# Three real products for each complex one in a gated mix of a state-space scan and a long convolution: products, one spectrum and the work between them moved

## The chip, the cores and the metric

The kernel runs on one core of one Trainium2 chip. The time of a run is the device time of one execution in microseconds (us). Three runs of the kernel before took 379.05, 379.08 and 380.93 us, so its median is 379.08 us.

## The reference, cut to what matters

Two sequence models read the same input x (2048 steps of 1024 channels, bf16). Model A is a diagonal complex state-space scan; model B is a causal convolution of each channel with a kernel as long as the sequence. A gate mixes them.

```python
def _A_ref(x, Lambda_re, Lambda_im, B_re, B_im, C_re, C_im, log_dt, Dskip):
    ...
    Bu = jnp.einsum("bld,pd->blp", x + 0j, B_bar)
    for t in range(L):
        h = Lam_bar[None, :] * h + Bu[:, t, :]
    ...
    y = 2.0 * jnp.einsum("blp,dp->bld", hseq, Cmat).real + x * Dskip[None, None, :]

def _B_ref(q, k, v, shift_k, ssm_k, ssm_D):
    for t in range(ks):
        k_shift = k_shift + k_pad[:, t:t + S, :] * shift_k[:, ks - 1 - t][None, None, :]
    kv = k_shift * v
    ...
    y_f = kv_f * kf_f[None, :, :, :]
    y = irfft2(y_f)[:, 0, :S, :].astype(bfloat16)
    y = y + kv * ssm_D[None, None, :]
    return q * y

g = _sigmoid((x * gate_w).sum(-1, keepdims=True))
return g * _A_ref(x, ...) + (1 - g) * _B_ref(x, k, v, ...)
```

The change concerns `kv_f * kf_f`, the product of two complex spectra in model B.

## The kernel before

**Model B by chunks.** The 1024 channels are cut into 8 chunks of 128 (`NC` = 8). For each chunk the convolution kernel (K) and the sequence kv (V) are cut into four blocks of 512 steps, and each block is taken to a spectrum of 512 frequencies by TensorE, as matmuls with tables of cosines (`CF`) and sines (`SF`, `NCF`). A spectrum tile has 128 partitions and, on each, [part c: cosine or sine][block b: 4][frequency and channel: 512], 4096 bf16 values. `fwd_K` (line 636) makes K's spectrum (PSUM tile `psk`, copied by ScalarE into a tile called BT) and `fwd_V` (line 674) makes V's (`psv`, copied into `Vh`); each does so in four pieces (`fi`), each with its own PSUM tile and one copy by ScalarE. K's spectrum needs each block to be overlapped with the block before it. For chunks 0 to 6 that is done by TensorE: 16 more matmuls with 384 columns. For chunk 7 (`c == NC - 1`) these are left out and VectorE does it in `overlap_K` (line 667) with six additions of 512 elements.

**The products.** Block b of the result is the sum over a of K(a) times V(b - a), complex, so there are 4 + 3 + 2 + 1 complex products for each frequency. `products` (line 687) is a generator, and each `yield` ends a step that the main loop places. It makes four real products for each complex one: both parts of K times both parts of V, in `acc`, `wkh` (`WK`) and a scratch tile `t`, then adds them up. A part of the sums (128x3072 elements, 768 KB) is added by a DMA with an accumulating write, issued from GpSimd's queue (`gather`, line 127: `acc<-wkh`), except in chunk 7. At its end it writes the result as sum and difference of two halves back into the place of V's spectrum (`Vh<-acc`, two instructions). `inverse` (line 769) is TensorE's inverse transform of it (`psz`): the first eight matmuls wait for the first of the two `Vh` instructions, the next eight for the second. ScalarE copies `psz` to `cv`, which goes to DRAM.

**The rest of a chunk.** `taps` (four-tap filter on TensorE), `times_v` (line 603; three steps: VectorE multiplies `ks` by v; TensorE mirrors it and ScalarE copies the mirror to `lo`; VectorE makes `ev<-ks,lo` and GpSimd's queue issues an accumulating DMA `ks<-lo`), and folds of K (`foldk`, or `mirror_K` for chunks 2 and 7). `fwd_V` needs `ev` in its first two matmuls of a piece and the landed `ks<-lo` in the next two.

**Model A between them.** `Bu` makes tiles of B times x. For the first four calls they are spread over the chunks as filler for TensorE by `parts` (line 1187): `Bu_tile` (calls 0 and 1; steps `odd`, `even`, then a step `lamd` that writes once more into the PSUM tile of `even`) and `Bu_halves` (calls 2 and 3; `odd`, `even`, and a step that does nothing). An `odd` or `even` step is 16 matmuls of 256 columns. After the chunks come the other calls, the scans on VectorE and the products with C (`psy`) on TensorE.

**What sets the order.** The helpers `mm`, `tt`, `act`, `move`, `gather` chain each instruction behind the one before it on its engine, so every engine runs in the order of the program's text, and the main loop (line 1190, `for c in range(NC - 1)`) is that order written out. In iteration c the order is, roughly: the inverse of chunk c - 1, the first steps of `products(c)`, K's spectrum of chunk c + 1, the fold and taps of chunk c + 2, the rest of `products(c)`, V's spectrum of chunk c + 1. PSUM is one pool of four tiles (line 82): a matmul group waits until ScalarE has copied out the tile that had its place.

All engine instructions issued through the helpers bear line 95 in the profile, so tiles are told apart by name.

Of the kernel before, what the change touches and what calls it, by code (L numbers as in the profile page):

```python
# [9 lines left out]
ALU = mybir.AluOpType  # L10
# [10 lines left out]
def kernel(  # L21
# [42 lines left out]
    NC = D // 128  # L64
# [33 lines left out]
    def mm(o, l, r, first, last):  # L98
        put("pe", nc.tensor.matmul, o, lhsT=l, rhs=r, start=first, stop=last)
# [587 lines left out]
    def products(c, h=0, home=u4, by_dma=True):  # L687

        K, Vt = (x[c][h].rearrange("p c b f d -> p c b (f d)") for x in (KH, VH))
        w = K.shape[3]  # L690
        A = sums[:, :, h * 2048:h * 2048 + 8 * w].rearrange("p k (c b x) -> p k c b x", c=2, x=w)

        def mult(a, t):

            if len(t.shape) == 2:
                t = t.rearrange("p (k y) -> p k y", k=2)
            t = t.rearrange("p k (c b x) -> p k c b x", c=2, x=w)
            k_ = bc(K[:, :, a:a + 1], [128, 2, 8 - 2 * a, w])
            v_ = bc(Vt[:, :, 0:4 - a].rearrange("p c b x -> p c (b x)")[:, None], [128, 2, 2, (4 - a) * w])
            tt(t, k_, v_, ALU.mult)  # L700
            return t

        n1 = WK[:, h * 3072:h * 3072 + 12 * w].rearrange("p (k c b x) -> p k c b x", k=2, c=2, b=3)

        def first(k):

            for f in range(2 if c == 0 and h == 0 else 1):
                x = slice(f * 128, f * 128 + 128) if c == 0 and h == 0 else slice(0, w)
# [5 lines left out]
        if by_dma:  # L714
            first(0)
            yield
            second(0)
            gather(A[:, 0, :, 1:], n1[:, 0])
            yield
            first(1)  # L720
            yield
            second(1)
            if c > 0:
                yield
            tt(A[:, 1, :, 1:], A[:, 1, :, 1:], n1[:, 1], ALU.add)
        else:
            mult(0, sums)
            yield
            mult(1, WK[:, 0:6144])
            yield  # L730
            tt(A[:, :, :, 1:], A[:, :, :, 1:], n1, ALU.add)
        if c > 0:
            yield
        if c > 0:
            n3 = mult(3, home([128, 4 * w], BF16, "t"))
            n2 = WK[:, 3072:7168].rearrange("p (k c b x) -> p k c b x", k=2, c=2, b=2)
            for k in (1, 0):
                tt(n2[:, k], bc(K[:, k:k + 1, 2:3], [128, 2, 2, w]), Vt[:, :, 0:2], ALU.mult)
            yield
            for k in (1, 0):  # L740
                tt(n2[:, k, :, 1:], n2[:, k, :, 1:], n3[:, k], ALU.add)
            tt(A[:, 1, :, 2:], A[:, 1, :, 2:], n2[:, 1], ALU.add)
            yield
            for i in (0, 1):
                tt(A[:, 0, i, 2:], A[:, 0, i, 2:], n2[:, 0, i], ALU.add)
            yield
        else:
            n2 = mult(2, home([128, 8 * w], BF16, "t"))
            n3 = mult(3, home([128, 4 * w], BF16, "t"))
            yield  # L750
            tt(n2[:, :, :, 1:], n2[:, :, :, 1:], n3, ALU.add)
            tt(A[:, 1, :, 2:], A[:, 1, :, 2:], n2[:, 1], ALU.add)
            yield
            tt(A[:, 0, :, 2:], A[:, 0, :, 2:], n2[:, 0], ALU.add)
            yield
        tt(A[:, 1, 1], A[:, 0, 0], A[:, 1, 1], ALU.subtract)
        tt(A[:, 1, 0], A[:, 0, 1], A[:, 1, 0], ALU.add)
        if c == 0 and h == 0:
            return
        t2 = sums[:, 1]  # L760
        if c > 0:
            lo, hi = (A[:, 1, :, :, i * 256:(i + 1) * 256] for i in range(2))
        else:
            lo, hi = (t2[:, i * 2048:(i + 1) * 2048].rearrange("p (c b x) -> p c b x", c=2, x=256) for i in range(2))
# [400 lines left out]
    step(turns)  # L1165
    taps(1, dg1)
    step(columns)
    p0 = products(0, 0)
    steps(p0, 3)
    run(columns)  # L1170
    step(sp)
# [12 lines left out]
            load_t(CT[pi][:, c], src[:, pi * 128:(pi + 1) * 128])  # L1184

    old = none
    parts = (None for i in range(4) for b in Bu(i) for _ in b)
    tiles = (b for i in (4, 5) for b in Bu(i))

    for c in range(NC - 1):  # L1190
        n, nn = c + 1, c + 2
        if c == 0:
            load("kn", 2)
            load("kT", 2)
            load("v", 2)
            load_BT(0, 0)
            load_xT(0, (0,))
            p1 = products(0, 1)
# [24 lines left out]
            run(apart)  # L1223
            continue
# [9 lines left out]
        if c == 6:  # L1234
            step(parts)
        run(back)
        step(tv)
        steps(prod, 4)
# [10 lines left out]
        if c == 2:  # L1249
            step(parts)  # L1250
        fwd_K(n, (0, 1))
        if c in (2, 6):
            step(parts)
        fwd_K(n, (2, 3))
        if c == 1:
            lam_diag(0, lam_pool, True)
        if c == 4:
            step(parts)
        if c == 6:
            run(sp)  # L1260
            s5p["Q"] = s5p["wu"]
# [3 lines left out]
        if nn < NC:  # L1265
            if not by_channel(nn):
                fk = mirror_K(nn)
            step(fk)
            if c < 5:
                step(fk)  # L1270
            if c == 4:
                step(parts)
            if c == 1:
                load_BT(1, 0, True)
            elif c < 5:
                load("v", nn, True)
            step(parts)
            taps(nn, dg)
            if c == 5:
                load("v", nn)  # L1280
                load_xT(2, held=True)
            if nn + 1 < NC:
                load("kT", nn + 1, True)
                load("kn", nn + 1)
                apart = spread(nn + 1)
                step(apart)
                if c == 1:
                    load_BT(1, 1)
                elif c in (2, 3):
                    load_xT(1, (3 - c,))  # L1290
                run(apart)
        step(prod)
        run(fk)
        run(prod)
        if n == NC - 1:
            overlap_K(n)
        if nn < NC:
            tv = times_v(nn)
            step(tv)
            step(parts)  # L1300
        else:
            run(next(tiles))
            CT[0] = ld.tile([128, 2, D], BF16, name="CTa", tag="ld")
# [4 lines left out]
            run(next(tiles))  # L1308
            run(next(tiles))
        fwd_V(n, (0, 1))  # L1310
        if c < 6 and c != 4:
            step(parts)
            if c in (1, 3):
                step(parts)
        fwd_V(n, (2, 3))
        if c in (4, 5):
            step(parts)
        if c == 1:
            lam_diag(1, lam_pool)
        old = tabs  # L1320
# [291 lines left out]
```

## Time and profile before

| | |
|---|---|
| three runs | 379.08 us median (379.05 to 380.93) |
| the profiled execution's own time | 381.19 us |
| its span, first to last instruction | 379.4 us |
| mean granted TensorE clock | 0.998 |
| TensorE (PE) busy | 373.6 us, 2469 matmuls |
| VectorE (DVE) busy | 368.0 us, 596 instructions |
| ScalarE (ACT) busy | 303.6 us, 465 instructions |
| GpSimd (POOL) busy | 78.0 us, 106 instructions |

A row of a timeline gives start, duration, engine, line, operation, output and inputs, shape and count, and in brackets the idle time before it with what ended it. A row of the chain of waits gives start, duration and what. A row of the groups gives the group with its count, then its busy time in us and the mean duration of one in ns. Matmuls overlap in a pipeline, so the distance between starts tells their rate, and not their durations. A row of DMA issues gives the transfer, the queue, the count, the size and the time from the issue to landing. The profiled execution took 1.8 us more than its span.

### The profile page before, as it was taken

What the parts mean: (1) busy time and instruction counts of PE and PEld (TensorE: products, weight loads), DVE (VectorE), ACT (ScalarE), POOL (GpSimd) and SP (SyncE); (2) the same over time, 40 slices, a digit from 0 to 9 for tenths busy, and PEclk for the clock granted to TensorE, in tenths of its full rate; (3) what the DMA queues carried; (4) which work ended last, traced back from release to release, by engine and by line L of the source; (5) the groups of instructions that cost most, each with busy time, mean ns of one, the idle gap of its engine ahead of it and who ended that gap; (6) DMA issues with size and microseconds to landing.
All of it is one profiled execution on the core that took longest, in us unless ns stands there. A gap on an engine that the chain in (4) does not pass through costs nothing.

```text
span 379.4 us, 6680 instructions
## 1 busy us (share of the span) xinstructions
PE 373.6 (98%) x2469; PEld 202.4 (53%) x2469; DVE 368.0 (97%) x596; ACT 303.6 (80%) x465; POOL 78.0 (21%) x106
## 2 busy tenths in 40 slices
PE   8999999999999999999999999999999999999996
PEld 5666457566584756754454444444445444444444
DVE  8899999999999999999999999999999999999984
ACT  5779998998989999777999699977979968936301
POOL 4011020020301102022012014122426322532000
PEclk9999999999999999999999999999999999999999
DMA  7879999999999998999999999946999998997223
GB/s 168 162 117 232 209 210 209 226 214 212 223 191 193 214 192 177 187 208 151 188 209 226 228 199 246 211 70 119 185 248 157 268 248 178 189 244 125 57 83 111
DMA packets 125827, 70.99 MB, mean 187 GB/s; under 512 B 104601, under 2 KB 107553, under 8 KB 125794
## 3 DMA queue, kind: packets, MB, share of 16 engines
q1 hardware_dynamic: 112416, 45.90, 55.4%
q0 software_dynamic: 12256, 24.38, 37.8%
q10 hardware_dynamic: 1122, 0.28, 0.4%
q8 instruction: 19, 0.31, 0.3%
q14 instruction: 14, 0.11, 0.1%
HBM read 15.48 MB, written 8.39 MB: 63 GB/s over the span
## 4 chain that ended last, share of the span: by engine, by line
PE 91%; DMA 6%; ACT 2%; SPq 0%; issue 0%; DVE 0%; ACTq 0%
PE psy L95 29%; PE both L95 22%; PE psk L95 10%; PE taps L95 6%; PE psv L95 6%; PE psz L95 5%; PE even L95 4%; PE odd L95 3%; DMA kT<-in_B_k_dram 3%; PE foldk L95 3%; DMA kT<-kT 2%; DMA kB<-kT 1%; ACT Vh L95 1%; PE p L95 1%; PE mirror L95 1%; ACT hr L95 1%
## 5 line engine op out<-in xcount | busy, mean ns | idle before, releaser
L95 PE MATMUL psy<-CT,U 128*128 128x512 bf16 (+1 forms) x426 | 93.2, 374 | 0.0
L95 PEld LDWEIGHTS <-U 128*128 128x128 bf16 x492 | 48.1, 98 | 55.6 <-issue 0.3
L95 PEld LDWEIGHTS <-BT 128*128 128x128 bf16 x544 | 50.5, 98 | 33.5 <-issue 0.2
L95 DVE TENSOR_TENSOR wkh<-BT,Vh 128x2048 bf16<-128x2048 bf16 (+3 forms) x31 | 44.7, 1460 | 0.0
L95 POOL DMA_DIRECT2D U<-Q x26 | 27.1, 1053 | 82.8 <-ACT Q L95 24.8
L95 DVE TENSOR_TENSOR acc<-BT,Vh 128x4096 bf16<-128x4096 bf16 (+3 forms) x19 | 37.0, 1950 | 0.6 <-ACT Vh L95 0.6
L95 ACT ACTIVATE Q<-U,lam 128x512 bf16<-128x512 bf16 (+1 forms) x60 | 35.0, 626 | 2.6 <-issue 1.9
L95 PE MATMUL both<-xT,BT 128*128 128x512 bf16 x160 | 35.3, 379 | 0.0
L95 ACT ACTIVATE Vh<-psv 128x1024 bf16<-128x1024 f32 x32 | 30.7, 1032 | 5.6 <-PE psv L95 5.6
L95 DVE TENSOR_TENSOR_SCAN A<-rv,init,A 128x256 bf16<-128x256 f32 x48 | 34.4, 736 | 0.0
L95 DVE TENSOR_TENSOR acc<-acc,wkh 128x1024 bf16<-128x1024 bf16 (+4 forms) x30 | 32.7, 1130 | 0.1
L95 ACT ACTIVATE BT<-psk 128x1024 bf16<-128x1024 f32 x31 | 30.1, 1037 | 2.3 <-PE psk L95 2.2
L95 ACT ACTIVATE U<-both 128x512 bf16<-128x512 f32 x44 | 24.3, 594 | 8.1 <-PE both L95 7.8
L95 POOL DMA_DIRECT2D acc<-wkh x8 | 9.8, 1219 | 100.2 <-DVE wkh L95 100.2
L95 PE MATMUL psk<-eok,SF 128*128 128x384 bf16 (+1 forms) x120 | 28.5, 354 | 0.0
L95 PEld LDWEIGHTS <-SF 128*128 128x128 bf16 x184 | 18.0, 98 | 18.8
L95 ACT ACTIVATE BT<-psy,gcols 128x1024 bf16<-128x1024 f32 (+1 forms) x6 | 6.3, 1043 | 24.7 <-issue 14.0
L95 PE MATMUL taps<-dg,kT 128*128 128x128 bf16 (+1 forms) x352 | 23.3, 219 | 1.0 <-DMA kT<-kT 0.5
L95 PE MATMUL psz<-Vh,CI 128*128 128x512 bf16 x64 | 24.3, 379 | 0.0
L95 PE MATMUL psz<-Vh,SI 128*128 128x512 bf16 x64 | 24.3, 379 | 0.0
L95 PEld LDWEIGHTS <-kT 128*128 128x128 bf16 x352 | 22.8, 104 | 2.7 <-DMA kT<-in_B_k_dram 1.4
L95 DVE TENSOR_TENSOR U<-U,trn 128x512 bf16<-128x512 bf16 (+1 forms) x60 | 22.0, 391 | 0.1
(225 smaller groups left out, 784.0 us busy)
## 6 DMA issues: line engine op xcount, KB each, us to landing
U<-Q POOLq DMA_DIRECT2D x26, 256.0 KB, 5.2
acc<-wkh POOLq DMA_DIRECT2D x6, 768.0 KB, 8.3
cv_scr<-cv SPq DMA_DIRECT2D x16, 256.0 KB, 3.7
kn<-in_B_ssm_k_dram SPq DMA_DIRECT2D x5, 512.0 KB, 4.4
v<-in_B_v_dram SPq DMA_DIRECT2D x5, 512.0 KB, 5.0
out_dram<-m SPq DMA_DIRECT2D x8, 256.0 KB, 4.6
BT<-cv_scr SPq DMA_DIRECT2D x7, 256.0 KB, 7.2
out_dram<-BT SPq DMA_DIRECT2D x7, 256.0 KB, 2.0
```

Of the source, the lines that this page charges most:

```text
L95: i = f(*a, **kw)
```

## The change

For chunks 1 to 7, `products` makes three real products for each complex one. With V's parts V0 and V1 and K's parts K0 and K1: `both[0]` is K0 (V1 - V0), `both[1]` is K1 (V1 + V0) and `third` is (K0 + K1) V0. The parts of the result are `third - both[1]` and `third + both[0]`. It first makes `Vp` (V1 - V0 and V1 + V0) in `WK`, and uses V1's place in `Vh` as scratch once V1 has been used. `products_0` keeps the old code for chunk 0.

K's spectrum of chunk 3 is made without the 16 overlapping matmuls too (`apart_K`), and `overlap_K` is two additions of 1536 elements that write into `WK` (`K_later`) instead of six of 512 in place. It runs before the last step but one of `products(c)`, not behind it, and for these two chunks the second product goes to the place of K's spectrum, which for chunk 3 is then the DMA's source (chunk 7 has no such DMA).

`times_v(nn)`'s first step (`ks<-ks,v`) comes before the last two steps of `products(c)`, not behind them. `in_parts` drops the steps that do nothing and takes the third call's tiles in the order odd, odd, even, even. The table `count` places the steps: chunk 1 as before, chunk 2 seven steps (before: five), chunks 3, 4 and 5 three each (before: four, five, four), chunk 6 none (before: two).

```diff
+    apart_K = (3, NC - 1)
+    K_later = {}
...
-                    mm(ps[:, cc], tab[:, mt, fsl], eo[:, cc, mt], mt == 0, c == NC - 1 and mt == 1)
-                for mt in range(0 if c == NC - 1 else 2):
+                    mm(ps[:, cc], tab[:, mt, fsl], eo[:, cc, mt], mt == 0, c in apart_K and mt == 1)
+                for mt in range(0 if c in apart_K else 2):
...
-        K = KH[c][0]
-        for b in (3, 2, 1):
-            tt(K[:, 0, b], K[:, 0, b], K[:, 1, b - 1], ALU.add)
-            tt(K[:, 1, b], K[:, 1, b], K[:, 0, b - 1], ALU.subtract)
+        K = KH[c][0].rearrange("p c b f d -> p c b (f d)")
+        t = K_later[c] = WK[:, 4096:7168].rearrange("p (c b x) -> p c b x", c=2, b=3)
+        tt(t[:, 0], K[:, 0, 1:], K[:, 1, 0:3], ALU.add)
+        tt(t[:, 1], K[:, 1, 1:], K[:, 0, 0:3], ALU.subtract)
...
+    def products(c, home=u4, by_dma=True):
...
+        both, third, S = blocks(area[:, 0:4096], 4, 2), blocks(area[:, 4096:6144], 4), blocks(area[:, 6144:], 4)
+        Vp = blocks(WK[:, 0:4096], 4, 2)
+        n1 = blocks(WK[:, 4096:], 3, 2)
+        free = Vt[:, 1].rearrange("p b x -> p (b x)")
+        m1, n2 = blocks(free[:, 0:1536], 3), blocks(free, 2, 2)
+        V0 = Vt[:, 0]
...
+        if c in K_later:
+            n1, later = K[:, :, 1:], K_later[c]
+            def Kb(b):
+                return later[:, :, b - 1:b] if b else K[:, :, 0:1]
+        def pair(o, b, n):
+            tt(o, bc(Kb(b), [128, 2, n, w]), Vp[:, :, 0:n], ALU.mult)
+        def one(o, b, n):
+            tt(o, bc(S[:, b:b + 1], [128, n, w]), V0[:, 0:n], ALU.mult)
+        tt(Vp[:, 1], Vt[:, 1], Vt[:, 0], ALU.add)
+        tt(Vp[:, 0], Vt[:, 1], Vt[:, 0], ALU.subtract)
+        yield
+        pair(both, 0, 4)
+        yield
+        pair(n1, 1, 3)
+        if by_dma:
+            gather(both[:, :, 1:], n1)
+        if c in K_later:
+            tt(S[:, 0], K[:, 0, 0], K[:, 1, 0], ALU.add)
+            tt(S[:, 1:], later[:, 0], later[:, 1], ALU.add)
+        else:
+            tt(S, K[:, 0], K[:, 1], ALU.add)
+        yield
+        t = home([128, 4 * w], BF16, "t")
+        n3, m2, m3 = blocks(t[:, 0:1024], 1, 2), blocks(t[:, 1024:], 2), S[:, 0:1]
+        pair(n3, 3, 1)
+        one(third, 0, 4)
+        yield
+        one(m1, 1, 3)
+        one(m2, 2, 2)
+        if not by_dma:
+            tt(both[:, :, 1:], both[:, :, 1:], n1, ALU.add)
+        one(m3, 3, 1)
+        tt(third[:, 1:], third[:, 1:], m1, ALU.add)
+        yield
+        pair(n2, 2, 2)
+        tt(m2[:, 1:], m2[:, 1:], m3, ALU.add)
+        tt(n2[:, :, 1:], n2[:, :, 1:], n3, ALU.add)
+        tt(third[:, 2:], third[:, 2:], m2, ALU.add)
+        yield
+        tt(both[:, :, 2:], both[:, :, 2:], n2, ALU.add)
+        yield
+        tt(both[:, 1], third, both[:, 1], ALU.subtract)
+        tt(both[:, 0], third, both[:, 0], ALU.add)
...
-    parts = (None for i in range(4) for b in Bu(i) for _ in b)
+    def in_parts():
+        for i in range(4):
+            for b in ([tile_ for pair_ in [Bu(2)] for _ in range(2) for tile_ in pair_] if i == 2 else Bu(i)):
+                for _ in range(1 if i == 2 else 3 if i < 2 else 2):
+                    step(b)
+                    yield
+    parts = in_parts()
+    count = {1: "D1 F1 G2", 2: "A1 B1 C1 D1 E2 F1", 3: "A1 D1 F1", 4: "C1 D1 F1", 5: "D1 F1 H1"}
+    def at(place):
+        for x in count.get(c, "").split():
+            if x[0] == place:
+                steps(parts, int(x[1:]))
...
+        at("A")
         fwd_K(n, (0, 1))
+        at("B")
         fwd_K(n, (2, 3))
...
+        at("C")
...
+            at("D")
             taps(nn, dg)
+            at("E")
...
         run(fk)
-        run(prod)
-        if n == NC - 1:
-            overlap_K(n)
         if nn < NC:
             tv = times_v(nn)
             step(tv)
-            step(parts)
+        step(prod)
+        if n in apart_K:
+            overlap_K(n)
+        run(prod)
+        if nn < NC:
+            at("F")
...
         fwd_V(n, (0, 1))
+        at("G")
         fwd_V(n, (2, 3))
+        at("H")
...
-    prod, back = products(c, 0, room, False), inverse(c - 1)
+    prod, back = products(c, room, False), inverse(c - 1)
     run(old)
-    steps(prod, 3)
+    steps(prod, 4)
```

More of the change, by code (lines that the diff above doesn't have):

```diff
@@ L685, in fwd_V, with products_0 @@
             act(of_tile(VH[c], fi), ps, func=ACT.Copy, scale=2.0 / 1024.0)
-    def products(c, h=0, home=u4, by_dma=True):
+    def products_0(h):
+        c = 0
         K, Vt = (x[c][h].rearrange("p c b f d -> p c b (f d)") for x in (KH, VH))
@@ L705, in first @@
         def first(k):
-            for f in range(2 if c == 0 and h == 0 else 1):
-                x = slice(f * 128, f * 128 + 128) if c == 0 and h == 0 else slice(0, w)
+            for f in range(2 if h == 0 else 1):
+                x = slice(f * 128, f * 128 + 128) if h == 0 else slice(0, w)
                 tt(A[:, k, :, :, x], bc(K[:, k:k + 1, 0:1, x], [128, 2, 4, x.stop - x.start]), Vt[:, :, :, x], ALU.mult)
@@ L712, in second @@
             tt(n1[:, k], bc(K[:, k:k + 1, 1:2], [128, 2, 3, w]), Vt[:, :, 0:3], ALU.mult)
[L714 to L755, printed above, removed]
+        first(0)
@@ new lines, in products_0 @@
+        yield
+        second(0)
+        gather(A[:, 0, :, 1:], n1[:, 0])
+        yield
+        first(1)
+        yield
+        second(1)
+        tt(A[:, 1, :, 1:], A[:, 1, :, 1:], n1[:, 1], ALU.add)
+        n2 = mult(2, u4([128, 8 * w], BF16, "t"))
+        n3 = mult(3, u4([128, 4 * w], BF16, "t"))
+        yield
+        tt(n2[:, :, :, 1:], n2[:, :, :, 1:], n3, ALU.add)
+        tt(A[:, 1, :, 2:], A[:, 1, :, 2:], n2[:, 1], ALU.add)
+        yield
+        tt(A[:, 0, :, 2:], A[:, 0, :, 2:], n2[:, 0], ALU.add)
@@ L756, in products @@
+        yield
         tt(A[:, 1, 1], A[:, 0, 0], A[:, 1, 1], ALU.subtract)
         tt(A[:, 1, 0], A[:, 0, 1], A[:, 1, 0], ALU.add)
-        if c == 0 and h == 0:
+        if h == 0:
             return
         t2 = sums[:, 1]
-        if c > 0:
-            lo, hi = (A[:, 1, :, :, i * 256:(i + 1) * 256] for i in range(2))
-        else:
-            lo, hi = (t2[:, i * 2048:(i + 1) * 2048].rearrange("p (c b x) -> p c b x", c=2, x=256) for i in range(2))
+        lo, hi = (t2[:, i * 2048:(i + 1) * 2048].rearrange("p (c b x) -> p c b x", c=2, x=256) for i in range(2))
@@ L1167 @@
     step(columns)
-    p0 = products(0, 0)
+    p0 = products_0(0)
     steps(p0, 3)
@@ L1197 @@
             load_xT(0, (0,))
-            p1 = products(0, 1)
+            p1 = products_0(1)
             fwd_K(n, (0, 1))
@@ L1256 @@
             lam_diag(0, lam_pool, True)
-        if c == 4:
-            step(parts)
+        at("C")
         if c == 6:
@@ L1270 @@
                 step(fk)
-            if c == 4:
-                step(parts)
             if c == 1:
@@ L1299 @@
             step(tv)
-            step(parts)
+        step(prod)
[4 more added lines that the diff above has]
+            at("F")
         else:
@@ L1310 @@
         fwd_V(n, (0, 1))
[L1311 to L1314, printed above, removed]
+        at("G")
         fwd_V(n, (2, 3))
-        if c in (4, 5):
-            step(parts)
+        at("H")
         if c == 1:
```

23 lines of the change are left out of this document (17 added, 6 removed).

## The prediction, made before the changed kernel was run

> **What bounds the kernel now.** I read the page's busy shares first, then the chain of waits, then timelines by engine where the two busiest engines meet.
>
> ```profile
> PE 373.6 (98%) x2469; PEld 202.4 (53%) x2469; DVE 368.0 (97%) x596; ACT 303.6 (80%) x465; POOL 78.0 (21%) x106
> PE 91%; DMA 6%; ACT 2%; SPq 0%; issue 0%; DVE 0%; ACTq 0%
> ```
>
> The chain that ended last is 91% TensorE, and VectorE is 97% busy: two engines are full, so a gain needs both. TensorE's order behind chunk 5 is untouched, so the question is when it gets there. The places where it meets VectorE are the inverse transforms: their first matmul (call its start P of chunk c) waits for the first of the two `Vh<-acc` instructions.
>
> ```profile
> 47.11 2.29 DVE L95 TENSOR_TENSOR acc<-BT,Vh 128x4096 bf16<-128x4096 bf16 x1
> 49.31 1.75 DVE L95 TENSOR_TENSOR wkh<-BT,Vh 128x3072 bf16<-128x3072 bf16 x1
> ...
> 64.07 2.35 DVE L95 TENSOR_TENSOR acc<-acc 128x2048 bf16<-128x2048 bf16 x2
> 66.46 2.36 DVE L95 TENSOR_TENSOR Vh<-acc 128x2048 bf16<-128x2048 bf16 x2
> 68.73 1.22 DVE L95 TENSOR_TENSOR ks<-ks,v 128x2048 bf16<-128x2048 bf16 x1
> ...
> 90.20 2.36 DVE L95 TENSOR_TENSOR Vh<-acc 128x2048 bf16<-128x2048 bf16 x2
> ...
> 93.67 2.29 DVE L95 TENSOR_TENSOR acc<-BT,Vh 128x4096 bf16<-128x4096 bf16 x1
> ...
> 116.86 2.29 DVE L95 TENSOR_TENSOR acc<-BT,Vh 128x4096 bf16<-128x4096 bf16 x1 [0.34 <-ACT Vh L95]
> ...
> 139.68 2.29 DVE L95 TENSOR_TENSOR acc<-BT,Vh 128x4096 bf16<-128x4096 bf16 x1
> ...
> 159.64 2.36 DVE L95 TENSOR_TENSOR Vh<-acc 128x2048 bf16<-128x2048 bf16 x2
> ```
>
> ```profile
> 68.76 0.38 PE L95 MATMUL psz<-Vh,CI 128*128 128x512 bf16 x1
> 92.20 0.38 PE L95 MATMUL psz<-Vh,CI 128*128 128x512 bf16 x1
> 115.55 0.38 PE L95 MATMUL psz<-Vh,CI 128*128 128x512 bf16 x1
> 138.26 0.38 PE L95 MATMUL psz<-Vh,CI 128*128 128x512 bf16 x1
> 161.21 0.38 PE L95 MATMUL psz<-Vh,CI 128*128 128x512 bf16 x1
> ```
>
> With one 2048 instruction at 1.22, the first half is ready at 67.68, 91.42 and 160.86 for P at 68.76, 92.20 and 161.21: slack 1.08, 0.78 and 0.35. TensorE is never held there now, but hardly ahead of being held. There is also a loop: the products of chunk c start when ScalarE has copied the last piece of V's spectrum, made just ahead of P of the chunk before. The starts 93.67, 116.86 and 139.68 lie 1.47, 1.31 and 1.42 behind P; take 1.4.
>
> **TensorE's own work.** The 16 matmuls with 384 columns:
>
> ```profile
> 104.72 1.75 PE odd L95 x16
> ...
> 142.31 6.05 PE psk L95 x32
> ...
> 165.25 3.45 PE psk L95 x16
> ```
>
> A spectrum with them takes 6.05, without 3.45: 2.60 less. That would be the gain if nothing waited. The dropped `Bu` steps hold no instruction; an `odd` or `even` step is 1.75. Chunk 2 gets two more of them: -2.60 + 3.50 = +0.90 at P2. Chunk 3 has one fewer ahead of its P (-0.85 in all at P3), chunk 4 the same number (-0.85), chunk 5 one fewer (-2.60 at P5 and ever after). TensorE's distances were 23.35, 22.71 and 22.95 (from P2 to P3, P4, P5); they become 21.60, 22.71 and 21.20 if it waits for nothing.
>
> **VectorE's work per chunk.**
>
> ```profile
> L95 DVE TENSOR_TENSOR wkh<-BT,Vh 128x1536 bf16<-128x1536 bf16 x4 | 3.8, 951 | 0.0
> L95 DVE TENSOR_TENSOR ev<-ks,lo 128x1024 bf16<-128x1024 bf16 x7 | 4.8, 685 | 0.0
> L95 DVE TENSOR_TENSOR BT<-BT 128x512 bf16<-128x512 bf16 x6 | 2.3, 420 | 0.1
> ```
>
> The new instructions have operations and sizes of the old: 4096 at 2.29, 3072 at 1.75, 2048 at 1.22, 1536 at 0.95, 1024 at 0.69, 512 at 0.42. Neighbours that do not depend on each other start 0.09 before the other's end (47.11 + 2.29 against 49.31); one that reads what its neighbour wrote starts 0.04 behind it (64.07 + 2.35 against 66.46). From the start of the products to the first `Vh<-acc`, the new order has one 4096, one 3072, nine 2048 (`ks<-ks,v` among them), two 1536, five 1024 (with `ev`) and two 512, twenty in all: 21.2. Twenty overlaps of 0.09 take off 1.8, four neighbours that depend add 0.12 each: 19.9. The old order took 66.46 - 47.11 = 19.35. So a chunk as a whole is shorter by some 0.6 (the old order had `ks`, 1.13, still to come behind `Vh`), but the result is ready 0.55 **later** in it. In chunk 1 that is hidden by the 1.08 of slack. The overlap of chunk 3's spectrum, 2 x 0.95 less the 0.2 of overlaps, falls into chunk 2 ahead of `Vh`: 21.6 there, so from a start 0.5 earlier than 90.20 - 19.35 its first half is ready at 93.2, hidden as long as P2 moves by 1.0 or more (below).
>
> A page speaks to the overlap: the Trainium skill, "VectorE: DVE Perf Modes", section "The DRAIN you can't avoid", says that the next operation does not start before the pipe is empty, and that a semaphore between two costs nothing. By it every new instruction would cost its whole duration, about 0.2 more per chunk than in the sum here. The rows above differ, with the 0.09 and the 0.04, and I go by them.
>
> **The loop with that.** From P of one chunk to P of the next VectorE needs at least 1.4 + 19.9 + 1.22 + 0.05 = 22.6 (before: 22.0). In chunk 5 one more 1024 (`eok`) comes in, 23.2. So the 21.60 and 21.20 that TensorE asks for cannot be had: the distances become 22.6, 22.7 and 23.2, in sum 0.5 less than the 69.0 of before, in place of 3.5 less.
>
> **ScalarE in chunk 2.** Shorter matmul groups meet the same copies.
>
> ```profile
> 74.39 0.59 PE L95 MATMUL psk<-eok,CF 128*128 128x512 bf16 x2
> ...
> 73.17 1.92 ACT L95 ACTIVATE cv<-psz 128x1024 bf16<-128x1024 f32 x2
> ...
> 77.78 1.94 ACT L95 ACTIVATE BT<-psk 128x1024 bf16<-128x1024 f32 x2
> ...
> 97.82 4.70 PE psk L95 x24
> ```
>
> Four PSUM tiles: one is held by `even` until its `lamd` copy, so the fourth piece of chunk 3's spectrum needs the first one's copy, which ScalarE ends at 77.78 + 0.97 = 78.75 behind two `cv`, a `lo`, four `dg` and another `lo`. TensorE now gets there at 74.39 + 3 x 0.86 + 0.44 (`lamd`) = 77.41: a wait of 1.3. Bounds: nothing, if ScalarE gets ahead, to the whole 2.6 that was saved. Then chunk 3's `lamd` comes behind the inverse and the mirror, so one PSUM tile is held through all of it, and the next spectrum's first piece waits for the first `cv` copy: 97.82 - 92.20 = 5.6 behind P2, where before only its second piece did. That costs up to 1.3, but stays inside the 22.6 - 21.6 = 1.0 that P3 waits for VectorE anyway, but for 0.3 at most. If that cover goes, 1.0 of it is seen.
>
> **The DMA behind the products.** In GpSimd's queue `acc<-wkh` stands ahead of `ks<-lo`, and the first lands first.
>
> ```profile
> 51.36 1.20 POOL L95 DMA_DIRECT2D acc<-wkh  x1 [14.69 <-DVE wkh L95]
> 55.84 0.91 POOL L95 DMA_DIRECT2D ks<-lo  x1 [3.28 <-DVE ev L95]
> ```
>
> ```profile
> acc<-wkh POOLq DMA_DIRECT2D x1, 768.0 KB, 9.3
> ks<-lo POOLq DMA_DIRECT2D x1, 256.0 KB, 7.1
> ```
>
> ```profile
> 63.55 0.59 PE L95 MATMUL psv<-ks,SF 128*128 128x512 bf16 x2
> ...
> 154.69 0.59 PE L95 MATMUL psv<-ks,SF 128*128 128x512 bf16 x2
> ...
> 148.41 0.90 POOL L95 DMA_DIRECT2D ks<-lo  x1 [3.27 <-PE psk L95]
> ...
> ks<-lo POOLq DMA_DIRECT2D x1, 256.0 KB, 6.2
> ```
>
> The source was written at 49.31 + 1.75; now two `Vp` additions come ahead of it, 2.4 later in the chunk. Chunk 1: the first landed at 60.66, the second at 62.94, 0.6 before TensorE wanted it. Moved 2.4 it would hold TensorE 1.8; if the transfers are quicker there, nothing. I take 0.3, nearer to nothing, because the other queue's traffic is older by then. Chunk 5: `ks<-lo` landed at 154.61 and was wanted at 154.69. Moved by 2.4 against its own chunk, it holds TensorE 2.3, so P5 comes 22.95 - 1.75 + 2.3 = 23.5 behind P4, 0.3 above VectorE's 23.2. Bounds for that 0.3: nothing, to 1.5 with a landing as slow as chunk 1's 7.1 and `acc` slower too. VectorE itself needs the sum of `acc` 16.3 into the chunk, and 6.3 + 0.3 + 9.3 = 15.9: hidden by 0.4; a landing as slow as that and 0.4 more would hold VectorE.
>
> **The sum.** P2: 0.9 + 1.3 + 0.3 = +2.5. P3: 22.6 for 23.35, -0.75. P4: 0. P5: 23.5 for 22.95, +0.55. Together **+2.3**, and TensorE's order behind it is the old one, so this stays to the end: span 379.4 to 381.7, and the median 379.08 to 381.4. (The profiled execution itself took 381.19, so its own time would be 383.5; the lowest of the three runs stands 0.03 below the median.) Without the terms of ScalarE and DMA it is 0.9 - 0.5 = +0.4.
>
> **Rivals.**
> - TensorE's work decides: the gain of 2.60 stays, 376.5. For it: the chain is 91% TensorE. Against: P5 would have to come 3.5 earlier against P2, from the slack of 0.35. It decides if the new products reach `Vh` within 19 of their start, as they would if dependent neighbours cost nothing and small instructions less. This one ends faster than before.
> - Only the loop counts, ScalarE's and the DMA's waits hidden: +0.4, 379.5. For it: ScalarE is 80% busy, so it has room somewhere. Against: its order ahead of that copy is fixed.
> - The DMA of chunk 1 in full: 1.5 more, 382.9. For it: the first row of its kind landed after 9.3.
> - A lowered clock: the new TensorE waits are longer than any of before in the chunks. The first row below has the clock, and the other two bound the cost:
>
> ```profile
> core 0: 379.4 us, clock 0.998
> ```
>
> ```profile
> 4.84 5.97 PE taps L95 x64
> ...
> 18.28 3.57 PE taps L95 x64
> ```
>
> The same 64 matmuls took 2.4 more at the start, at most all by the clock: 383.8. The Trainium skill, "TensorE: Matmul & The Clock Gate", section "A second HAM failure mode: psum-queue depth-cycling", says that short TensorE pauses between groups that cycle through PSUM tiles can switch the clock down. The kernel before cycles so, and its clock stays up.
>
> **How the numbers follow.** Chances: the sum 0.50 (of it 0.16 below +1.9), TensorE's work 0.19, the loop alone 0.15, the first DMA in full 0.13, the clock 0.03. This measurement tells about 0.5%, 1.9 us, from no change. Slower by more: 0.34 + 0.13 + 0.03 = 0.50; within: 0.16 + 0.15 + 0.02 = 0.33; faster: 0.17. For eight in ten: from 376.8, just above TensorE's work alone, to 383.2, above the first DMA in full; the sum's own range is 379.8 to 382.6.
>
> **What would show it.** P2 at about 94.7, with a wait of some 1.3 ahead of the last piece of chunk 3's spectrum; the start of chunk 4's spectrum behind a `cv`; VectorE idle ahead of the products of chunk 3 by over 1, ended by ScalarE's `Vh`; P5 near 163.5, with `psv<-ks` held by a DMA; busy PE lower by the 16 matmuls, busy DVE by about 2. I am wrong if P5 comes at 159 or so, or if the distance of P behind the products' start is under 21.

## The result and the profile after

The changed kernel took 400.21, 401.79, 407.29 and 407.44 us, a median of 404.54; four runs of the kernel before beside it had a median of 380.0. The ratio is 1.056, with a 95% interval of 1.048 to 1.065. This ratio and every one below leaves out runs more than 1.5% above the fastest of their kernel, here the two of 407, and the profiles of the products alone, of `lo` first and of dg later (below) are of such longer runs. The profiled execution took 401.79, with a span of 400.0 and a mean granted clock of 0.982. So the change costs some 20 us, where the prediction had 2.3.

The page of the changed kernel, in its order: busy shares, granted clock by slice, the chain that ended last, and one of the costliest groups (busy time and mean ns of one, then the idle time ahead of it).

```profile
PE 374.1 (94%) x2419; PEld 200.6 (50%) x2453; DVE 365.8 (91%) x620; ACT 304.5 (76%) x465; POOL 76.7 (19%) x106
...
PEclk9999999998998998989999999999999999999999
...
PE 54%; DVE 19%; DMA 9%; ACT 7%; SPq 6%; issue 4%; DVEq 0%; ACTq 0%
...
L95 DVE TENSOR_TENSOR ks<-ks,v 128x2048 bf16<-128x2048 bf16 x7 | 8.5, 1216 | 18.3 <-DMA v<-in_B_v_dram 13.6
```

VectorE has 2.2 us less to do, as forecast, but both engines now wait, the chain is only 54% TensorE, and 9% of it is DMA. One group has nearly the whole of it: VectorE sat idle for 18.3 us ahead of `ks<-ks,v`. The groups of the kernel before have for the same instruction:

```profile
L95 DVE TENSOR_TENSOR ks<-ks,v 128x2048 bf16<-128x2048 bf16 x7 | 8.5, 1212 | 0.0
```

VectorE's timeline of the changed kernel (start, duration, what, and in brackets the idle time before it with what ended it) shows where:

```profile
87.69 1.22 DVE L95 TENSOR_TENSOR ks<-ks,v 128x2048 bf16<-128x2048 bf16 x1 [3.59 <-DMA v<-in_B_v_dram]
...
117.16 1.23 DVE L95 TENSOR_TENSOR ks<-ks,v 128x2048 bf16<-128x2048 bf16 x1 [5.43 <-DMA v<-in_B_v_dram]
...
144.07 1.23 DVE L95 TENSOR_TENSOR ks<-ks,v 128x2048 bf16<-128x2048 bf16 x1 [4.55 <-DMA v<-in_B_v_dram]
...
171.71 1.23 DVE L95 TENSOR_TENSOR ks<-ks,v 128x2048 bf16<-128x2048 bf16 x1 [4.68 <-ACT Vh L95]
```

Four waits, one in each of chunks 2 to 5. The last bears the name of ScalarE's `Vh`, which `ks` does not read; that name is only the latest semaphore event. Of the two inputs of `ks`, the copy of the taps had ended at 167.15, so the wait must have been for the transfer of v issued at 166.06 (below), though the trace does not have its landing. Now SyncE's queue, which issues that transfer, and ScalarE's, which lets it go:

```profile
83.02 0.38 SPq L95 DMA_DIRECT2D v<-in_B_v_dram  x1
...
110.77 0.38 SPq L95 DMA_DIRECT2D v<-in_B_v_dram  x1
...
139.67 0.38 SPq L95 DMA_DIRECT2D v<-in_B_v_dram  x1
...
166.06 0.39 SPq L95 DMA_DIRECT2D v<-in_B_v_dram  x1
```

```profile
108.48 2.17 ACT L95 ACTIVATE eok<-foldk 128x1024 bf16<-128x1024 f32 x2
110.55 0.20 ACT L95 ACTIVATE v<-pih 128x1 bf16<-128x1 f32 x1
```

`load("v", nn, True)` first has ScalarE write one column of v's place (`hold`, the `v<-pih`), and that write stands in ScalarE's queue behind the two copies of the fold, which come late in the chunk. The transfer is issued as that write ends (110.55 + 0.20, then 110.77) and `ks` starts 4.4 to 6.4 later. In the kernel before the issue was as late, but nobody wanted v so early. Its SyncE timeline, its DMA issues (the last number is the median time to landing) and its VectorE timeline:

```profile
84.29 0.38 SPq L95 DMA_DIRECT2D v<-in_B_v_dram  x1
```

```profile
v<-in_B_v_dram SPq DMA_DIRECT2D x5, 512.0 KB, 5.0
```

```profile
92.47 1.22 DVE L95 TENSOR_TENSOR ks<-ks,v 128x2048 bf16<-128x2048 bf16 x1
```

There v landed at 89.3 and `ks` ran at 92.47, behind `Vh`: 3.2 of slack. The change wants it two steps of the products earlier, and a VectorE that waits at `ks` holds all that stands behind it, the two `Vh` among it, and so TensorE. TensorE's timeline of the changed kernel, and its windows over the `psz` that follow (length, busy time and count, granted clock, DMA share, GB/s):

```profile
95.37 0.61 PE L95 MATMUL psz<-Vh,CI 128*128 128x512 bf16 x1 [2.53 <-DVE Vh L95]
...
123.23 0.61 PE L95 MATMUL psz<-Vh,CI 128*128 128x512 bf16 x1 [4.82 <-DVE Vh L95]
...
150.14 0.61 PE L95 MATMUL psz<-Vh,CI 128*128 128x512 bf16 x1 [2.83 <-DVE Vh L95]
...
177.78 0.61 PE L95 MATMUL psz<-Vh,CI 128*128 128x512 bf16 x1 [4.74 <-DVE Vh L95]
```

```profile
95.37:100.44 5.07, 5.07 (x16) 0.68 1.07 191
123.23:128.03 4.80, 4.80 (x17) 0.71 0.93 149
150.14:155.13 4.99, 4.99 (x16) 0.69 0.63 132
177.78:182.50 4.72, 4.72 (x16) 0.70 0.39 85
```

The waits make 14.9 in sum. Behind each of them the clock is low for a while, and a `psz` that took 3.45 takes 4.7 to 5.1: 5.8 more in the four.

**The loop.** With P for the first `psz` of a chunk (66.86 for chunk 1), the distance to the next P is made of three pieces: P to the issue of v, the issue to the start of `ks`, and `ks` to the next P. They are 16.16 + 4.67 + 7.68, 15.40 + 6.39 + 6.07, 16.44 + 4.40 + 6.07 and 15.92 + 5.65 + 6.07. That is 28.5, 27.9, 26.9 and 27.6, in place of 23.4, 23.4, 22.7 and 23.0. The first piece is tied to P by the order of the text (mirror, spectrum, fold, copies, hold), so a late P makes the next v late.

**Where the 20.6 lies.** The spans differ by 400.0 - 379.4. Up to P of chunk 1 the changed kernel is 1.9 ahead (a start that differs between executions, below); chunks 2 to 5 cost 110.92 - 92.45 = 18.5; from there to the last `psz` another 1.4 (the fourth low clock); behind it 2.6. That last piece is this wait, and SyncE's issue of a load (`pbb`) ahead of it:

```profile
271.04 1.02 PE L95 MATMUL psy<-CTa,U 128*128 128x512 bf16 x4 [2.47 <-ACT U L95]
```

```profile
232.88 7.11 SPq L95 DMA_TRANSPOSE CT<-in_A_C_im_dram  x1
...
251.68 1.23 SPq L95 DMA_DIRECT2D pbb<-cv_scr  x1
```

`pbb` stands in SyncE's queue behind transposing loads of `CT`, and the issue of one of them holds the queue for 7.11. The same load in the kernel before:

```profile
216.18 1.30 SPq L95 DMA_TRANSPOSE CT<-in_A_C_im_dram  x1
```

### The profile page after: what moved, and what is told of

It reads as the page before. It is cut to its first block, busy times and chain, and to the rows that moved or that the text cites. A ratio compares the mean times of both kernels' runs of the same rounds, so it can differ in the third digit from the quotient of the medians.

```text
span 400.0 us, 6631 instructions
## 1 busy us (share of the span) xinstructions
PE 374.1 (94%) x2419; PEld 200.6 (50%) x2453; DVE 365.8 (91%) x620; ACT 304.5 (76%) x465; POOL 76.7 (19%) x106
## 4 chain that ended last, share of the span: by engine, by line
PE 54%; DVE 19%; DMA 9%; ACT 7%; SPq 6%; issue 4%; DVEq 0%; ACTq 0%
PE psy L95 28%; DVE acc L95 9%; PE psk L95 6%; PE both L95 6%; SPq L95 6%; DMA v<-in_B_v_dram 5%; PE psz L95 5%; DVE Vh L95 3%; DVE wkh L95 3%; PE taps L95 3%; PE foldk L95 2%; DVE t L95 2%; DMA ks<-lo 1%; DMA pbb<-cv_scr 1%; ACT Vh L95 1%
## 5 line engine op out<-in xcount | busy, mean ns | idle before, releaser
L95 PE MATMUL psz<-Vh,CI 128*128 128x512 bf16 x64 | 28.0, 437 | 14.9 <-DVE Vh L95 14.9
L95 POOL DMA_DIRECT2D U<-Q x26 | 25.3, 987 | 84.6 <-ACT Q L95 26.2
L95 ACT ACTIVATE cv<-psz 128x1024 bf16<-128x1024 f32 x16 | 16.1, 1019 | 20.1 <-PE psz L95 20.0
L95 POOL DMA_DIRECT2D acc<-wkh x7 | 8.5, 1221 | 103.5 <-DVE wkh L95 103.5
L95 PE MATMUL psz<-Vh,SI 128*128 128x512 bf16 x64 | 27.6, 431 | 0.0
L95 PE MATMUL psk<-eok,SF 128*128 128x512 bf16 (+1 forms) x111 | 26.9, 356 | 0.3
L95 DVE TENSOR_TENSOR acc<-acc,Vh 128x2048 bf16<-128x2048 bf16 (+2 forms) x28 | 26.0, 950 | 0.0
L95 DVE TENSOR_TENSOR ks<-ks,v 128x2048 bf16<-128x2048 bf16 x7 | 8.5, 1216 | 18.3 <-DMA v<-in_B_v_dram 13.6
L95 PEld LDWEIGHTS <-kT 128*128 128x128 bf16 x352 | 21.5, 101 | 1.6 <-DMA kT<-in_B_k_dram 1.2
L95 PE MATMUL taps<-dg,kT 128*128 128x128 bf16 (+1 forms) x352 | 22.0, 212 | 0.3 <-DMA kT<-in_B_k_dram 0.3
```

The lines of the kernel that those rows point to most:

```text
L95: i = f(*a, **kw)
```

## The experiments

The theory is the late load: `ks` was moved ahead of its input. The rival is that the new code costs: more and smaller instructions, the spectrum on VectorE, the steps of `Bu`.

**ks behind the products again.**

```diff
         run(fk)
-        if nn < NC:
-            tv = times_v(nn)
-            step(tv)
         step(prod)
...
         run(prod)
         if nn < NC:
+            tv = times_v(nn)
+            step(tv)
             at("F")
```

> The changed kernel with one thing undone: ks<-ks,v (first step of times_v) stands behind the end of the products again, as before the change. Theory (the late load): in the changed kernel ks waits for the transfer of v (3.6, 5.4, 4.6 and 4.7 us in chunks 2 to 5, 18.3 in sum) and everything behind it on VectorE, the two Vh among it, waits too; with ks behind Vh that wait is hidden again, psz comes at distances of 21.5 to 23.5 as in the prediction, and the time is 377 to 383. Rival (the new code): the three real products, the spectrum on VectorE or the moved steps of Bu are what costs; then the time stays above 395. In between, 384 to 395, both have a part.

The ratio to the kernel before is 1.004 (0.998 to 1.009), the lowest run 381.39: nearly the whole loss is gone with one instruction moved back. Chunks 2 and 5 took 25.81 and 25.53, outside the 21.5 to 23.5 that was expected. What is left there, in its TensorE timeline and windows, are the waits that the prediction had priced:

```profile
76.35 0.59 PE L95 MATMUL psk<-eok,CF 128*128 128x512 bf16 x2 [1.27 <-ACT BT L95]
...
97.63 0.59 PE L95 MATMUL psk<-eok,CF 128*128 128x512 bf16 x2 [1.08 <-ACT cv L95]
...
156.46 1.00 PE L95 MATMUL psv<-ks,SF 128*128 128x512 bf16 x2 [2.50 <-DMA ks<-lo]
```

```profile
156.40:160.00 3.60, 3.54 (x9) 0.53 1.06 199
```

**ks ahead, in the kernel before.** Nothing of the new code is in this one.

```diff
         run(fk)
+        step(prod)
+        if nn < NC:
+            tv = times_v(nn)
+            step(tv)
         run(prod)
         if n == NC - 1:
             overlap_K(n)
         if nn < NC:
-            tv = times_v(nn)
-            step(tv)
             step(parts)
```

> The kernel before with only ks<-ks,v put ahead of the last two steps of the products. Theory (the late load): v landed 20.6 us behind the psz of the chunk before (89.4 against 68.76) and is then followed by ks 1.2, two acc 2.4, the first Vh 1.2 and some start, so that the distance from psz to psz becomes 25 to 26 in place of 23, four times over: 388 to 396, with VectorE idle ahead of ks by 1 to 4 us and the idle time ended by the transfer of v. Rival (the new code costs, not this move): 379 to 382.

Ratio 1.029 (1.021 to 1.036), median 395.31. VectorE's timeline:

```profile
88.61 1.22 DVE L95 TENSOR_TENSOR ks<-ks,v 128x2048 bf16<-128x2048 bf16 x1 [2.97 <-DMA v<-in_B_v_dram]
...
115.26 1.23 DVE L95 TENSOR_TENSOR ks<-ks,v 128x2048 bf16<-128x2048 bf16 x1 [3.79 <-DMA v<-in_B_v_dram]
...
140.76 1.22 DVE L95 TENSOR_TENSOR ks<-ks,v 128x2048 bf16<-128x2048 bf16 x1 [2.66 <-DMA v<-in_B_v_dram]
...
167.67 1.23 DVE L95 TENSOR_TENSOR ks<-ks,v 128x2048 bf16<-128x2048 bf16 x1 [3.46 <-DMA v<-in_B_v_dram]
```

The move alone makes the same four waits in old code. Over chunks 2 to 5 it costs 13.3 (105.76 against 92.45), in the new code 14.3 (110.92 against 96.65). In the changed kernel the two additions of `overlap_K` stand between `ks` and `Vh` in chunk 2 (7.68 in place of 6.0), and v is issued some 0.8 later behind P. Another 2.6 of the difference lies behind the last `psz`, where this kernel has no wait for `U`.

**v early, ks where the change put it**, but for chunk 5, where `ks` goes behind the products.

```diff
+        if 2 <= c < 5:
+            load("v", nn)
         tabs, back, prod = turn_table(c - 1) if c <= NG else none, inverse(c - 1), products(c)
...
-            elif c < 5:
-                load("v", nn, True)
...
             tv = times_v(nn)
-            step(tv)
+            if c != 5:
+                step(tv)
...
         run(prod)
+        if c == 5:
+            step(tv)
```

> The changed kernel with the loads of v for chunks 4, 5 and 6 issued at the start of an iteration, ahead of cv and with no hold by ScalarE (their place in the buffer has been free for a chunk); chunk 7's v has no free place so early, and its ks goes behind the products. Theory (the late load): VectorE waits nowhere ahead of ks, and the time is 377 to 384, with ks ahead of Vh costing at most its own 1.1 a chunk against e1_ks_back. Rival (the place of ks in the order costs, whenever v lands): 392 or more.

Ratio 1.011 (1.006 to 1.016): most of the loss is back, 0.045 of 0.056. But VectorE still waits there, for the next of `ks`'s inputs, the copy of the taps by ScalarE (its timeline):

```profile
86.70 1.22 DVE L95 TENSOR_TENSOR ks<-ks,v 128x2048 bf16<-128x2048 bf16 x1 [2.43 <-ACT ks L95]
...
111.71 1.23 DVE L95 TENSOR_TENSOR ks<-ks,v 128x2048 bf16<-128x2048 bf16 x1 [0.97 <-ACT ks L95]
...
136.41 1.23 DVE L95 TENSOR_TENSOR ks<-ks,v 128x2048 bf16<-128x2048 bf16 x1 [2.35 <-ACT ks L95]
```

So the expectation that VectorE waits nowhere failed. In this order `ks` has two late inputs, and v was the later one.

**The three products alone**, in the kernel before: `products` and `overlap_K` of the change, with `apart_K = (NC - 1,)` and everything else as it was.

> The kernel before with only the three real products (chunks 1 to 7); chunk 3's spectrum by TensorE, the steps of Bu and ks as before. Theory (the late load): no transfer is wanted earlier than it was but the ks<-lo, which is issued 2.4 later: 378 to 382, VectorE's busy time lower by 5 to 8. Rival (the new code costs): 388 or more.

Ratio 1.005 (0.999 to 1.011). Chunks 2 to 4 have the distances of the kernel before to 0.01 (table below); the new products are hidden there. VectorE's busy time is 3.6 lower (364.4), not 5 to 8. Chunk 5 has 27.94 in place of 22.95, in this profile, by the DMA that they delay (TensorE's timeline), and by a clock of 0.55 in the 3.6 behind it:

```profile
156.73 0.68 PE L95 MATMUL psv<-ks,SF 128*128 128x512 bf16 x2 [3.15 <-DMA ks<-lo]
```

**The kernel before, once more.**

> The kernel before, unchanged, for a second profile of it: psz of chunk 0 began at 45.00 in the one profile and at 43.25 to 44.30 in the five profiles of other kernels, whose text up to there is the same. If that is a difference between executions, it comes at 43 to 44.5 here, with the distances of the chunks as before (23.4, 23.35, 22.7, 22.95), and the span is 378 to 379; if the changed kernels begin earlier, it comes at 45.

P of chunk 0 came at 43.80, so the 45.00 of the first profile is a difference between executions. The span was 380.1, not 378 to 379, with 24.88 for chunk 1 and 23.68 for chunk 5, the other three distances as before (in chunk 5 `psv` waited 0.80 for `ks<-lo`): one execution against another differs by a microsecond or so.

**TensorE kept busy in the wait.** Is the low clock behind the waits a cost of its own?

```diff
             ps = ps2([128, 2, 4, 128], "psz")
+            for _ in range(16 if par == 0 and 2 <= c <= 5 else 0):
+                mm(ps[:, 0], CI[:, 0, 0:128], CI[:, 0].rearrange("p (b d) -> p b d", d=128), True, True)
```

> The changed kernel with 16 matmuls of no use (CI times CI, 3.45 us in all) written into the first tile of psz ahead of its own in chunks 2 to 5, where TensorE waits 2.5 to 4.8 us for Vh; psz overwrites them. Theory (the clock has a part): TensorE no longer sits idle for 2.5 us at a stretch, so its granted clock, 0.60 in the 3.5 us behind the wait of chunk 3 in the changed kernel, stays near 1.0, psz takes 3.45 in place of 4.8 to 5.1, the four distances shrink by 1.3 to 1.6 each, and the time is 393 to 397, with 64 matmuls more. Rival (the waits of v are the whole cost, and the clock of a stretch that VectorE holds up anyway costs nothing): 400 or more.

Ratio 1.058 (1.050 to 1.066), the same as the changed kernel. The windows over the `psz` of chunks 3 and 4 have the clock that was wanted:

```profile
122.30:125.80 3.50, 3.48 (x17) 1.00 1.05 161
149.80:153.30 3.50, 3.46 (x17) 1.00 0.37 75
```

No time came of it. v was issued 13.8 and 15.1 behind P of chunks 2 and 3, in place of 15.4 and 16.4, but `ks` then began 6.7 and 6.4 behind the issue, in place of 6.4 and 4.4; in chunk 5 it was issued later (17.0, not 15.9), and there a wait of 3.30 still brought a clock of 0.50. In chunk 2 the 16 matmuls themselves ran some 0.4 past the end of the first `Vh` (95.27, P at 95.74). So 5.8 of low clock is not a term that can be taken off by itself: the transfer sets the end of the piece. Why the transfers took longer when they began earlier was not tried further.

**One chunk alone**: the first experiment, with `ks` ahead in chunk 3 only.

```diff
         if nn < NC:
             tv = times_v(nn)
-            step(tv)
+            if c == 3:
+                step(tv)
...
         if nn < NC:
+            if c != 3:
+                step(tv)
             at("F")
```

> e1_ks_back, with ks<-ks,v ahead of the last two steps of the products in chunk 3 alone. Theory (the load of v is issued a fixed 15 to 16 us behind the psz of the chunk before, lands some 5 later, and the next psz comes 6 behind that, so each chunk that asks early pays for itself, once): the distance of chunk 3 is 26 to 28 in place of 22.5, those of chunks 4 and 5 are those of e1_ks_back (22.8 and 25.5 or less), and the span is 4 to 5.5 longer than its 381.1. Rival (one late ks upsets the chunks behind it too, or is made up for by them): chunk 4 at 25 or more, or the sum of the four distances within 2 of 96.65.

Chunk 3 took 28.50, a little above the range. Chunk 4 took 24.95, not 22.8, just under the rival's 25. Chunk 5 took 22.17, 3.4 less than with `ks` behind: there `psv` waited 2.50 for `ks<-lo`, here 0.46, and no low clock followed. The sum of the four is 101.44, 4.8 above 96.65, and the span 387.2, 6.1 longer. TensorE's timeline and windows say what chunk 4 had:

```profile
121.19 0.61 PE L95 MATMUL psz<-Vh,CI 128*128 128x512 bf16 x1 [5.83 <-DVE Vh L95]
```

```profile
121.19:126.04 4.85, 4.85 (x12) 0.50 0.93 150
```

Half the clock for 4.85 us is up to 2.4 of matmul time, enough for the 2.1. Here, where `ks` is not early in the next chunk, the low clock is on the path. So the early `ks` costs its own chunk 6.0 and the next one 2.1, and chunk 5 gives 3.4 back; both parts of the expectation, that a chunk pays for itself alone and the size of it, missed.

**Four tries at a faster kernel**, the first two from the first experiment, the others each from the one before it. Chunk 5's wait for `ks<-lo`: by an earlier issue, and by an addition on VectorE.

```diff
-        steps(prod, 4)
+        steps(prod, 2 if c == 5 else 4)
         run(tv)
+        steps(prod, 2 if c == 5 else 0)
```

> e1_ks_back, with ev and the issue of ks<-lo ahead of the second product and of acc<-wkh in chunk 5 alone. In e1_ks_back psv waited 2.5 there for ks<-lo, and the clock was 0.53 for 3.6 us behind it. Theory (both are the price of a late ks<-lo, and of nothing else): the wait and the low clock go, the distance in chunk 5 falls from 25.53 to 21.5 to 23, and the time is 2.5 to 4 under that of e1_ks_back, 377 to 379 where the kernel before has 379. Rival (acc<-wkh, now issued 2 later, is late in its place and holds VectorE): the distance stays above 24.5 and the time with it.

Ratio 1.007 (1.003 to 1.010). The rival holds: the wait for `ks<-lo` is gone, and VectorE waits for the other DMA, which is now later:

```profile
159.24 1.23 DVE L95 TENSOR_TENSOR acc<-acc,Vh 128x2048 bf16<-128x2048 bf16 x1 [2.24 <-DMA acc<-wkh]
```

```diff
-        if c == 1:
+        if c in (1, 6):
             tt(ks[:, 2:4], ks[:, 2:4], lo, ALU.add)
```

> e1_ks_back, with lo added to ks by VectorE (one addition of 1024 elements, 0.7 us) in place of the DMA ks<-lo in chunk 5 alone. There psv waited 2.5 for that DMA, and the granted clock was 0.53 in the 3.6 us behind the wait, which makes 1.7 more. Theory (the wait brings the low clock with it, and both are on the path): the distance of psz in chunk 5 falls by 2.5 to 4.2, from 25.53 to 21.5 to 23, and the time is 2 to 4 under e1_ks_back, 377.5 to 380. Rival (VectorE's loop is the bound there by now): the distance stays above 24 and the time at that of e1_ks_back.

The distance fell from 25.53 to 22.89, that is 2.64, the wait and the low clock less 1.53 for `Vh`. The time was no better: 1.017 (1.010 to 1.023). In its profile more than that is lost behind the last `psz`: from there to the end are 171.8, not the 166.9 of `ks` behind. `psy` waits 2.82 for `U`, as in the changed kernel, and the clock is 0.50 for 3.41 behind the wait. There `pbb` was issued 24.4 behind the last `psz`; in the kernel before it was 14.0.

```diff
-    count = {1: "D1 F1 G2", 2: "A1 B1 C1 D1 E2 F1", 3: "A1 D1 F1", 4: "C1 D1 F1", 5: "D1 F1 H1"}
+    count = {1: "D1 F1 G2", 2: "A1 B1 C1 D1 E2", 3: "D2 F1", 4: "C1 D1 F1", 5: "D1 E1 F1 H1"}
```

> e8_lo_by_dve, with one step of Bu moved from chunk 2 to chunk 5 and the lamd of chunk 3 put behind its spectrum, so that no PSUM tile is held over it. Theory (TensorE's work decides where VectorE has room): chunk 2 falls by 1.75 to 24.0, chunk 3's wait for cv (1.08) goes and VectorE's 21.5 to 22 decides, chunk 5 is 22.9; in sum 0.5 to 1 below the kernel before, time 377.5 to 379.5. Rival (chunk 2 gets the whole 1.75 back as a longer wait for ScalarE's copy of psk): the same as e8_lo_by_dve.

Ratio 1.002 (0.999 to 1.005). Chunks 2 and 3 came as expected (24.07, 21.89). Chunk 5 took 24.59, not 22.9: TensorE got to the taps earlier, and another transfer was not there yet.

```profile
149.76 0.22 PE L95 MATMUL taps<-dg,kT 128*128 128x64 bf16 x2 [1.37 <-DMA kT<-kT]
```

Last, with `dgs(nn)` and the first step of `fold_columns` behind the first half of `fwd_K` in chunk 2:

> e9_steps_moved, with ScalarE's four dg and one lo<-kn put behind the first two copies of psk in chunk 2. In e1_ks_back the fourth piece of chunk 3's spectrum waited 1.27 for that copy. Theory (these five instructions, 1.85 us, are what the copy stands behind): the wait goes, chunk 2 falls by 1.2 to 22.8 to 23.3 (VectorE's bound with overlap_K is about 23.2), and the time is 376.5 to 378.5. Rival (lo and dg are then late in their places): no gain, or slower than e9_steps_moved.

Ratio 1.001 (0.997 to 1.005). Chunk 2 fell to 23.55, a little above the range, but its profile has 22.46, 23.27 and 23.61 for chunks 3 to 5. Neither of the two last ones can be told from the kernel before, and no version here beats it.

Distances from P to P, from the starts of the first `psz` in TensorE's timelines, and the ratio of the times:

| kernel | chunk 2 | 3 | 4 | 5 | sum | ratio |
|---|---|---|---|---|---|---|
| before | 23.44 | 23.35 | 22.71 | 22.95 | 92.45 | 1 |
| before, again | 23.44 | 23.35 | 22.72 | 23.68 | 93.19 | |
| changed | 28.51 | 27.86 | 26.91 | 27.64 | 110.92 | 1.056 |
| ks behind again | 25.81 | 22.49 | 22.82 | 25.53 | 96.65 | 1.004 |
| before, ks ahead | 26.68 | 26.64 | 25.51 | 26.93 | 105.76 | 1.029 |
| v early | 27.37 | 23.39 | 24.70 | 21.73 | 97.19 | 1.011 |
| products only | 23.43 | 23.35 | 22.72 | 27.94 | 97.44 | 1.005 |
| busy in the wait | 29.13 | 26.58 | 27.52 | 28.10 | 111.33 | 1.058 |
| ks ahead in chunk 3 | 25.82 | 28.50 | 24.95 | 22.17 | 101.44 | 1.022 |
| lo first | 25.81 | 22.50 | 22.83 | 25.27 | 96.41 | 1.007 |
| lo by VectorE | 25.82 | 22.50 | 22.82 | 22.89 | 94.03 | 1.017 |
| steps moved | 24.07 | 21.89 | 22.81 | 24.59 | 93.36 | 1.002 |
| dg later | 23.55 | 22.46 | 23.27 | 23.61 | 92.89 | 1.001 |

## Why the prediction was wrong

**The step that failed** is in "VectorE's work per chunk". There `ks<-ks,v` is one of "nine 2048", a duration of 1.22 that changes its place; the loop, "1.4 + 19.9 + 1.22 + 0.05 = 22.6", counts durations and overlaps alone. When `ks`'s inputs are ready was never looked up. The prediction did look at the DMAs that the moved work issues, `ks<-lo` and `acc<-wkh`, but not at one that it reads. In place of 22.6 the loop is 15.4 to 16.4 to the issue of v, 4.4 to 6.4 to `ks`, 6.1 (in chunk 2 7.7) to the next P. None of the rivals had this wait.

By its other steps:

- **Durations and overlaps of the new products.** 19.9 from the start to the first `Vh` was right: 45.55 to 65.55 in chunk 1 of the changed kernel, where v had long been there. Whole durations for all twenty would make 21.2. That they are hidden in chunks 2 to 4 is shown by the experiment with the products alone.
- **P2.** +0.9 for TensorE's steps and +1.3 for ScalarE's copy: the wait is 1.27 in both the changed kernel and the one with `ks` behind, whose chunk 2 is 2.37 longer than before, against 2.2. The 0.3 for a DMA of chunk 1 falls ahead of P of that chunk: `psv` waited 0.46 there in the changed kernel, and nothing with `ks` behind.
- **P3 and P4.** 22.49 and 22.82 with `ks` behind, against 22.6 and 22.7. The first is right for another reason: with `ks` out of the way VectorE's loop is shorter by its 1.1, and the wait of 1.08 for `cv`, which the prediction had hidden behind VectorE, is what decides.
- **P5.** The wait for `ks<-lo` is 2.50 with `ks` behind, against 2.3. The low clock behind it, which the step did not have, makes the distance 25.53 in place of 23.5. In the changed kernel the later `ks` gave that DMA the time to land.
- **The clock** was a rival of 0.03, on the ground that the kernel before keeps its clock up. It does; its waits are shorter. In the changed kernel the clock was low four times, but filling the waits brought nothing back, so it is a companion of the cause and not the cause.
- **VectorE's busy time** is lower by 2.2, against 2. TensorE's busy time rose by 0.5 in place of falling, since matmuls at half the clock count as longer.
- **The sum without the move.** Had `ks` stayed, +0.4% (-0.2 to +0.9) is what the rest of the change costs, and the +0.6% of the prediction lies in that interval. So the size that it gave belongs to the change without its moved step, and that is partly luck: in the profile of that kernel chunks 2 to 5 are 4.2 longer than before (96.65 against 92.45), where the prediction has 2.0, and a P of chunk 1 that comes 2.5 earlier (66.26 for 68.76) makes up for it.

What stays open is the last 2.6: `pbb` issued 21.3 behind the last `psz` and not 14.0, behind slower issues of `CT`, and `psy` waiting 2.5 for it by way of `U`. The same wait stands in the profiles of the products alone, of lo by VectorE and of dg later, and not in those of steps moved or of `ks` behind, whose order there is the same. It was not tried what sends an execution one way or the other.

## What to carry to other kernels

A moved instruction takes its inputs with it: for each of them compare the time at which it lands or is copied, in the trace of before, with the new start, loads that a hold issues just in time above all. Where the late input's own issue hangs on the loop, the difference is paid in every turn. And where one wait is taken away, look for the next late input behind it: here v, then the copy of the taps; `ks<-lo`, then `acc<-wkh`; the steps of `Bu`, then `kT`.

## What the runs showed of the clock

In the chunks, every TensorE wait of 2.13 us or more was followed by a stretch at half the granted clock, and every wait of 1.97 or less by none. But the length of the wait alone does not decide: behind the chunks, waits of 2.47 (changed) and 2.66 (products alone) were followed by the full clock, and one of 2.82 (lo by VectorE) by half.

The traces show what does. In the changed kernel the low stretches begin at 95.25, 122.56, 149.86 and 177.17 and last 3.41 each. From one to the next it is 27.31 each time, 8 times 3.41, though the waits did not end that regularly. In all thirteen profiles the times at which the clock changes, from its first rise on, lie whole steps of 3.41 apart, and a low stretch in the body of a kernel is one or two steps. TensorE's windows of the changed kernel, step by step, around the wait that ended at 95.37 and the one that ended at 271.04:

```profile
91.84:95.25 3.41, 0.99 (x5) 1.00 0.73 234
95.25:98.66 3.41, 3.29 (x8) 0.50 0.97 165
98.66:102.07 3.41, 3.41 (x20) 1.00 1.07 235
...
265.92:269.33 3.41, 2.60 (x12) 1.00 0.77 203
269.33:272.74 3.41, 1.70 (x8) 1.00 0.77 132
272.74:276.15 3.41, 3.41 (x17) 1.00 0.13 22
```

The first wait left TensorE idle for 2.42 of one step (3.41 less the 0.99 busy), and the next step has the half clock, which costs up to 1.7. The second fell into two steps, 0.81 and 1.71 idle, and none was lowered. Over all thirteen profiles each step at full clock with 2.09 or more idle was followed by a low one, and none with 1.87 or less was. So a wait counts by its share of one step. The longest that left the clock up in the chunks is this one of the kernel with v early, in TensorE's timeline and its windows:

```profile
117.78 0.39 PE L95 MATMUL psz<-Vh,CI 128*128 128x512 bf16 x1 [1.97 <-DVE Vh L95]
```

```profile
117.78:121.30 3.52, 3.52 (x17) 1.00 0.93 147
```

The Trainium skill, "TensorE: Matmul & The Clock Gate", section "HAM oscillation — how this bites in real kernels", warns of TensorE gaps over some 3.4 us, behind which matmuls start at half the clock. The half clock agrees with these rows; the length of the gap does not, since 2.13 sufficed here.
